# Starting a load-bound decode kernel: x and wq issued ahead of the start barrier, and the first key tile in two half loads behind fewer zero products

## The chip, the cores and the metric

The kernel runs on one core of one Trainium2 chip. Times are device microseconds (us) of a whole execution. The profile's span is about 1.4 us shorter than the time of the same execution. TensorE does the matrix products, VectorE and ScalarE copy, reduce and exponentiate, GpSimd fills constants, and SyncE issues nearly all loads, which 16 DMA engines carry out.

## The reference

```python
xn = layernorm(x)                                # x is [4, 1, 448]
s  = attention(xn, k_cache, v_cache, wq, wo)     # 16 query heads, 8 key/value heads, 8192 keys of 256
g  = silu(mlp_block(xn, w1, w2, w3, w4))         # with one token, the w1/w2 part is shifted out to zero
return x + s * g                                 # [4, 1, 448]
```

The caches are bfloat16 of shape [4, 8, 8192, 256]. So there are 32 tiles (batch, head), each with a key tile and a value tile of 4,194,304 bytes. The weights wq (3.67 MB), w3 and w4 (1.6 MB each) and wo (3.67 MB) come on top. Almost no arithmetic is done per byte.

## The kernel before

SyncE issues, in one queue: wq, w3, w4, key tiles 0 and 1, most of wo, then key tile 2, value tile 0, and so on. Key tile h waits until tile h-2 has been transposed (semaphore `v_k`), since it takes over its buffer. The first six loads, 18.0 MB, wait for nothing.

```python
def begin_ahead(nc, loads):             # moves these loads into the first block
    ...
    for load in reversed(loads):
        at = next(n for n, i in enumerate(first)
                  if i.engine == load.engine and isinstance(i, mybir.InstDrain))
        first.insert(at + 1, load)      # just behind the engine's drain of the start barrier

# SyncE
ahead.append(sp.sem_inc(S["pause"], 1)); ahead.append(take(sp, "pause"))
ahead.append(sp.dma_start(<wq>).then_inc(S["dwq"], 16))
...
load_k(0); load_k(1)
load_wo(NLATE, HQ, "dwo")
for h in range(2, NH):
    load_k(h)                           # waits for v_k >= h - 1
    load_v(h - 2)
# ScalarE
ahead.append(act.dma_start(x_sb[:, :], x2d).then_inc(S["dx"], 16))
```

TensorE first does the small layers (layernorm of x, then wq, w3, w4), then 14 products of zeros, which only keep it busy until key tile 0 has landed, then the tiles. A tile has 16 groups: 8 transposes of 128x128 (`f_t`), and three groups later the 8 score products (`f_s`). Its two tile bodies are a loop whose place in TensorE's program is set by `head_slot`, here 88.

```python
for i in range(NWARM):                  # 14
    pe.matmul(psv[0:PVW, 0:QW], pT[:, 0, 0:PVW], wq_sb[:, 0, 0:QW], start=True, stop=True)

def f_t(h, j):
    if j == 0:
        take(pe, "dk%d" % (h % 2), 16)  # the key tile has landed
    ...                                 # 8 transposes

with nc.Fori(0, 2, engines=[e]) as part:
    with nc.Fori(0, NH // 4, engines=[e], head_slot={e: 88}):
        body(0)
        body(1)
    with pe.If(part == 1):
        finish()
```

Of the kernel before, what the change touches and what calls it, by code (L numbers as in the profile page):

```python
# [12 lines left out]
P = 128  # L13
# [19 lines left out]
def begin_ahead(nc, loads):  # L33


    names = {i.name for i in loads}
    blocks = nc.main_func.blocks
    for b in blocks:
        rest = [i for i in b.instructions if i.name not in names]
        if len(rest) < len(b.instructions):  # L40
            b.instructions = rest
    first = blocks[0].instructions
    for load in reversed(loads):
        at = next(n for n, i in enumerate(first)
                  if i.engine == load.engine and isinstance(i, mybir.InstDrain))
        first.insert(at + 1, load)
    blocks[0].instructions = first


# [6 lines left out]
def bass_recurrent_scan__gqa_block_cached__mixer_s_mlp__decode_kernel(  # L56
# [32 lines left out]
    NCH = SK // P  # L89
# [5 lines left out]
    NGR = NCH // GC  # L95
# [15 lines left out]

    LATE = ((0, 1), (2,), (3,))
    NLATE = sum(len(g) for g in LATE)
    NWARM = 14
    ROW_PAD = 192
    TW = NHALF * REP
    OT_AHEAD = 3
# [3 lines left out]
    x2d = A_x.rearrange("b s d -> b (s d)")  # L121
# [3 lines left out]
    def where(h):  # L125
        return h // HKV, h % HKV

    with ExitStack() as es:
        def sb(name, shape, dty):
            return es.enter_context(nc.sbuf_tensor(name, shape, dty))  # L130

        align = sb("align", [P, ROW_PAD], BF16)
        kn = sb("kn", [P, 2, NCH, DH], BF16)
# [28 lines left out]
        x_sb = sb("x_sb", [Bn, D], BF16)  # L162
# [17 lines left out]
        psv = es.enter_context(nc.psum_tensor("psv", [P, 512], F32))  # L180

        S = {n: es.enter_context(nc.semaphore(n)) for n in (
            ["dx", "dwq", "dw3", "dw4", "dwo", "dk0", "dk1", "dv0", "dv1", "dout", "pause"]
            + ["dvl%d" % i for i in range(NPIECE)] + ["dwl%d" % i for i in range(len(LATE))]
            + ["p_td", "p_ta", "p_sc", "p_m1", "p_m2", "p_m3", "p_tr", "p_ou", "p_pv", "p_x", "p_q", "p_h", "p_h2", "p_o"]
            + ["v_ev", "a_ev", "v_rmax", "v_diag", "v_neg", "v_ot", "a_exp", "v_q", "g_c",
# [25 lines left out]
        def kn_dst(h):  # L212
            return kn[:, h % 2].rearrange("p c d -> p (c d)")

        def store(eng, i):
            eng.dma_start(out2d[:, i * DQ:(i + 1) * DQ], out_b[i * PQ:i * PQ + Bn, :]
                          ).then_inc(S["dout"], 16)

        def prog_sp(sp):
            ahead.append(sp.sem_inc(S["pause"], 1))  # L220
            ahead.append(take(sp, "pause"))
            ahead.append(sp.dma_start(
                vflat[1][:, 0:DK * HDH],
                A_wq.rearrange("d (t n) -> (d t) n", t=NHF).rearrange(
                    "(p j) n -> p (j n)", j=DK)).then_inc(S["dwq"], 16))
            sp.dma_start(vflat[0][:, 0:DK * FH],
                         B_w3.rearrange("d (t n) -> (d t) n", t=NHF).rearrange(
                             "(p j) n -> p (j n)", j=DK)).then_inc(S["dw3"], 16)
            sp.dma_start(w4_sb.rearrange("p a k n -> p a (k n)"),
                         B_w4.rearrange("(a p k) n -> p a (k n)", a=NHF, k=NFK)  # L230
                         ).then_inc(S["dw4"], 16)

            def load_k(h):
                b, g = where(h)
                if h >= 2:
                    sp.wait_ge(S["v_k"], h - 1)
                sp.dma_start(kn_dst(h), A_k_cache[b, g].rearrange("(p c) d -> p (c d)", p=P)
                             ).then_inc(S["dk%d" % (h % 2)], 16)

            def load_v(h):  # L240
                b, g = where(h)
                src = A_v_cache[b, g].rearrange("(p c) d -> p c d", p=P)
                if h < NH - 1:
                    sp.wait_ge(S["v_v"], h + 1)
                    sp.dma_start(vflat[h % 2], src.rearrange("p c d -> p (c d)")
                                 ).then_inc(S["dv%d" % (h % 2)], 16)
                else:

                    sp.wait_ge(S["v_k"], h)
                    for i in range(NPIECE):  # L250
                        lo, hi = PIECES[i], PIECES[i + 1]
                        sp.dma_start(
                            kn[:, 1 - h % 2, lo:hi, :].rearrange("p c d -> p (c d)"),
                            src[:, lo:hi, :].rearrange("p c d -> p (c d)")
                        ).then_inc(S["dvl%d" % i], 16)

            load_k(0)
            load_k(1)
            wo_src = A_wo.rearrange("(h p c) n -> p h (c n)", p=P, c=NHALF)

            def load_wo(lo, hi, sem):
                sp.dma_start(wo_sb[:, lo:hi].rearrange("p h c n -> p h (c n)"),
                             wo_src[:, lo:hi]).then_inc(S[sem], 16)

            load_wo(NLATE, HQ, "dwo")
            for h in range(2, NH):
                load_k(h)
                load_v(h - 2)
            load_v(NH - 2)
            load_v(NH - 1)  # L270
            for i, hs in enumerate(LATE):
                load_wo(hs[0], hs[-1] + 1, "dwl%d" % i)
            sp.wait_ge(S["v_out"], 1)
            store(sp, 0)
            take(sp, "dout", 16 * NDG)

        def take(eng, name, n=1):
            return eng.wait_ge(S[name], n).then_inc(S[name], -n)  # L278
# [23 lines left out]
        def evac(engine, h, j):  # L302
            take(engine, "p_td" if j in D_GROUPS else "p_ta")
            src = pst[j % NST][:].bitcast(BF16)
            dst = kT[:, j % RING, :]
            if j in D_GROUPS:
                engine.tensor_copy(dst, src).then_inc(S["v_ev"], 1)  # L307
            else:
                engine.activation(dst, src, ACT.Copy).then_inc(S["a_ev"], 1)  # L309

        def prog_act(act):
            ahead.append(act.dma_start(x_sb[:, :], x2d).then_inc(S["dx"], 16))
            c = _Chain(act, S["a_c"])
            for k, col in ((1, 0), (2, 8)):
                act.wait_ge(S["v_w"], k)
                c(act.activation(st[:, col + 2:col + 3], st[:, col + 1:col + 2], ACT.Sqrt))
            act.wait_ge(S["g_c"], NPC)
            for t in (vflat[1][:, DK * HDH:NCH * DH], vflat[0][:, DK * FH + NF * D:NCH * DH]):
                c(act.activation(t, pT[:, 0, 0:1].broadcast_to([P, t.shape[1]]), ACT.Copy))
            act.wait_ge(S["v_w"], 3)  # L320
            c(act.activation(gel_b[:, :], gel_a[:, :], ACT.Tanh))
            act.wait_ge(S["v_w"], 4)
            c(act.activation(sg4[:, :], bout[:, :], ACT.Tanh, scale=0.5))

            def exps(h):
                s = h % 2
                take(act, "v_neg")
                sc = psc[s][:, 0:NCH * REP].rearrange("p (k h) -> p k h", h=REP)
                pv_p = pT[:, s, 0:NCH * REP].rearrange("p (k h) -> p k h", h=REP)
                for hh in range(REP):  # L330
                    ins = act.activation(pv_p[:, :, hh], sc[:, :, hh], ACT.Exp,  # L331
                                         bias=negb[:, s, hh:hh + 1], scale=SCALE,
                                         accum_out=rowsum[:, s, hh:hh + 1])
                    if hh == REP - 1:
                        ins.then_inc(S["a_exp"], 1)

            with nc.Fori(0, NH // 2, engines=[mybir.EngineType.Activation]):
                for h in range(2):
                    for j in range(NGR):
                        if j not in D_GROUPS:  # L340
                            evac(act, h, j)
                        if j == J_BC + 2:
                            exps(h - 1)
            exps(NH - 1)
            act.wait_ge(S["v_out"], 1)
            store(act, 1)
# [200 lines left out]
        def prog_pe(pe, xn_mark, xn2_mark):  # L547
# [34 lines left out]
            for k in range(NFK):  # L582
                for a in range(NHF):
                    i = k * NHF + a
# [9 lines left out]

            for i in range(NWARM):
                pe.matmul(psv[0:PVW, 0:QW], pT[:, 0, 0:PVW], wq_sb[:, 0, 0:QW], start=True, stop=True)

            def f_t(h, j):
                if j == 0:
                    take(pe, "dk%d" % (h % 2), 16)  # L600
                dst = pst[j % NST][:].bitcast(BF16)
                for t in range(TB):
                    kl, half = divmod(t, NHALF)
                    ins = pe.transpose(dst[:, t * P:(t + 1) * P],  # L604
                                       kn[:, h % 2, GC * j + kl, half * P:(half + 1) * P],
                                       ident_b[:, :])
                ins.then_inc(S["p_td" if j in D_GROUPS else "p_ta"], 1)
# [70 lines left out]
            h = NH - 1  # L678
# [99 lines left out]
        marks, ahead = [], []  # L778
# [52 lines left out]
```

## Time and profile before

| what | value |
|---|---|
| time, median of the first 3 runs | 653.85 us (653.24 to 654.89) |
| span of the profiled run | 652.0 us |
| loaded from HBM | 279 MB, 428 GB/s over the span |
| TensorE busy, granted clock | 84%, 0.908 |

These are lines of the page. The DMA row gives, for 40 equal slices of the span, the busy share of the DMA engines in tenths (9 means 90% or more); the row below it gives GB/s.

```profile
span 652.0 us, 22813 instructions
...
DMA  9999999999999999999999999999999999999997
GB/s 374 440 420 433 430 434 434 430 438 426 440 426 440 426 440 426 440 428 436 432 435 430 434 434 426 440 426 440 426 440 428 438 428 438 430 436 430 434 429 301
```

The load stream is busy in every slice but part of the last. It is taken as the resource that bounds the kernel; run e7_2mb_less below tests that.

Next, the windows view at the start. The columns are the window, its length, the busy time of five engines, the TensorE clock, the busy share of the DMA engines and GB/s.

```profile
1.00:1.20 0.20, 0.00 (x0) 0.00 (x0) 0.20 (x1) 0.20 (x1) 0.07 (x1) 1.00 0.15 9
1.20:1.40 0.20, 0.00 (x0) 0.00 (x0) 0.20 (x1) 0.20 (x1) 0.10 (x1) 1.00 4.21 1008
...
2.20:2.40 0.20, 0.00 (x0) 0.00 (x0) 0.19 (x1) 0.00 (x0) 0.00 (x0) 1.00 0.00 0
```

The stream's packets begin at about 1.2 us (the 9 GB/s before that are x). A window books a packet whole where it starts. In this trace the first 16 packets of wq, 28 KB each, start between 1.26 and 2.12 us.

The timeline, from its parts for the start, for TensorE and for SyncE. Columns: start, length, engine, line, operation, out<-in, count, and in brackets the idle time just before and what ended it.

```profile
0.21 0.56 ACTq L312 DMA_DIRECT2D x_sb<-in_A_x_dram  x1
...
0.24 0.41 SPq L222 DMA_DIRECT2D vb<-in_A_wq_dram  x1
...
2.01 0.38 DVE L385 CAST x_f<-x_sb 4x448 f32<-4x448 bf16 x1 [0.60 <-DMA x_sb<-in_A_x_dram]
...
23.94 5.26 PE L596 MATMUL psv<-vb,pT 128*32 128x512 bf16 x14
30.07 1.05 PE L604 MATMUL pst<-ident_b,kn 128*128 128x128 bf16 x16 [0.87 <-PEq L278]
...
41.77 0.33 SPq L237 DMA_DIRECT2D kn<-in_A_k_cache_dram  x1
45.88 0.33 SPq L245 DMA_DIRECT2D vb<-in_A_v_cache_dram  x1
```

x is issued 0.03 us before wq; VectorE reads it at 2.0 us (L385). The zero products (L596) end at 29.2 us, and the first transposes (L604) start at 30.07 us after a pause of 0.87 us. Key tile 2 is issued at 41.77 us, value tile 0 at 45.88 us.

From the list of waits (total us, number, longest) and from the chain that ended last (start, length, what):

```profile
PE pst L604 <- PEq L278: 79.3, 29, 4.5
```

```profile
648.14 1.55 PE pst L703 x24
```

"PEq L278" is a semaphore wait in TensorE's own program; ahead of the first transpose of a tile (L604) it is the wait for the key tile. TensorE waits for key tiles in nearly every tile, 79.3 us in all. The execution ends with 24 output products, which wait for the last load of wo.

### The profile page before, as it was taken

What the parts mean: (1) busy time and instruction counts of PE and PEld (TensorE: products, weight loads), DVE (VectorE), ACT (ScalarE), POOL (GpSimd) and SP (SyncE); (2) the same over time, 40 slices, a digit from 0 to 9 for tenths busy, and PEclk for the clock granted to TensorE, in tenths of its full rate; (3) what the DMA queues carried; (4) which work ended last, traced back from release to release, by engine and by line L of the source; (5) the groups of instructions that cost most, each with busy time, mean ns of one, the idle gap of its engine ahead of it and who ended that gap; (6) DMA issues with size and microseconds to landing.
All of it is one profiled execution on the core that took longest, in us unless ns stands there. A gap on an engine that the chain in (4) does not pass through costs nothing. (4 is left out here: it accounts for less than half of the span.)

```text
span 652.0 us, 22813 instructions
## 1 busy us (share of the span) xinstructions
PE 550.5 (84%) x9937; PEld 470.7 (72%) x9937; DVE 276.9 (42%) x622; ACT 255.8 (39%) x364; POOL 3.6 (1%) x17
## 2 busy tenths in 40 slices
PE   2799997988887987888897888898888798878897
PEld 1487876987676876667787766787677688757774
DVE  7344544343343443434443444444344344434442
ACT  4144543443343443323443333444234344423440
POOL 2000000000000000000000000000000000000000
PEclk9998999888799898889987888988779987978999
DMA  9999999999999999999999999999999999999997
GB/s 374 440 420 433 430 434 434 430 438 426 440 426 440 426 440 426 440 428 436 432 435 430 434 434 426 440 426 440 426 440 428 438 428 438 430 436 430 434 429 301
DMA packets 12353, 279.13 MB, mean 428 GB/s; under 512 B 1204, under 2 KB 3256, under 8 KB 3768
## 3 DMA queue, kind: packets, MB, share of 16 engines
q1 hardware_dynamic: 12328, 278.99, 99.5%
q8 instruction: 7, 0.11, 0.1%
q10 hardware_dynamic: 16, 0.01, 0.0%
q14 instruction: 2, 0.02, 0.0%
HBM read 278.99 MB, written 0.00 MB: 428 GB/s over the span
## 5 line engine op out<-in xcount | busy, mean ns | idle before, releaser
L604 PE MATMUL pst<-ident_b,kn 128*128 128x128 bf16 x4096 | 342.7, 237 | 81.4 <-PEq L278 79.3
L309 ACT ACTIVATE kT<-pst 128x1024 bf16<-128x1024 bf16 x224 | 229.3, 1024 | 357.5 <-ACTq L278 356.3
L604 PEld LDWEIGHTS pst<-ident_b,kn 128*128 128x128 bf16 x4096 | 271.7, 107 | 87.2 <-issue 86.6
L307 DVE COPY kT<-pst 128x1024 bf16<-128x1024 bf16 x288 | 197.5, 691 | 261.1 <-DVEq L278 261.1
L616 PE MATMUL psc<-qc,kT 128*128 128x2 bf16 x4096 | 178.2, 164 | 0.0
L616 PEld LDWEIGHTS psc<-qc,kT 128*128 128x128 bf16 x4096 | 157.1, 98 | 28.7 <-issue 28.5
L655 PE MATMUL psv<-vb,pT 128*4 128x512 bf16 x1056 | 85.6, 378 | 0.0
L634 PE MATMUL psm<-sel,po 128*128 128x2 f32 x272 | 36.8, 257 | 0.5 <-PEq L278 0.5
L634 PEld LDWEIGHTS psm<-sel,po 128*128 128x128 f32 x272 | 34.8, 196 | 0.9 <-issue 0.9
L655 PEld LDWEIGHTS psv<-vb,pT 128*4 128x4 bf16 x1056 | 21.8, 82 | 15.0 <-issue 0.4
L466 DVE TENSOR_REDUCE rmax<-psc 128x2 f32<-128x128 f32 x32 | 9.3, 292 | 48.1 <-DVEq L278 48.1
L484 DVE COPY po<-psv 128x512 f32<-128x512 f32 x34 | 23.5, 691 | 4.0 <-DVEq L278 3.3
L331 ACT ACTIVATE pT<-psc,negb 128x64 bf16<-128x64 f32 x66 | 20.6, 332 | 5.4 <-ACTq L278 5.4
L471 DVE TENSOR_REDUCE gmax<-psm 2x1 f32<-2x128 f32 x32 | 8.9, 279 | 32.3 <-DVEq L278 32.3
L628 PEld LDWEIGHTS psm<-diag,ones_f 2*128 2x128 f32 x66 | 13.5, 253 | 6.3 <-issue 5.0
L628 PE MATMUL psm<-diag,ones_f 2*128 2x2 f32 x66 | 16.2, 313 | 1.1 <-PEq L278 0.9
L331 ACT ACTIVATION_READ_ACCUMULATOR pT<-psc,negb 128x1 f32 x66 | 13.6, 206 | 0.0
L624 PEld LDWEIGHTS psm<-ident_f,rmax 128*2 128x2 f32 x32 | 2.6, 80 | 14.0 <-issue 14.0
L646 PE MATMUL psm<-rowsum,ones_f 128*128 128x2 f32 x64 | 11.6, 251 | 0.0
L552 PE MATMUL pst<-ident_b,xn_b 4*128 4x4 bf16 x14 | 0.6, 161 | 11.5 <-DVE xn_b L379 6.8
L646 PEld LDWEIGHTS psm<-rowsum,ones_f 128*128 128x128 f32 x64 | 9.5, 188 | 0.0
L474 DVE TENSOR_SCALAR diag<-ident_f,gmax 2x2 f32<-2x2 f32 x32 | 6.9, 217 | 4.8 <-DVEq L278 1.1
(101 smaller groups left out, 101.1 us busy)
## 6 DMA issues: line engine op xcount, KB each, us to landing
kn<-in_A_k_cache_dram SPq DMA_DIRECT2D x32, 4096.0 KB, 25.5
vb<-in_A_v_cache_dram SPq DMA_DIRECT2D x31, 4096.0 KB, 30.5
vb<-in_A_wq_dram SPq DMA_DIRECT2D x1, 3584.0 KB, 11.4
vb<-in_B_w_dram SPq DMA_DIRECT2D x2, 1568.0 KB, 16.3
wo_sb<-in_A_wo_dram SPq DMA_DIRECT2D x1, 2688.0 KB, 43.3
kn<-in_A_v_cache_dram SPq DMA_DIRECT2D x1, 2048.0 KB, 24.7
kn<-in_A_v_cache_dram SPq DMA_DIRECT2D x1, 1024.0 KB, 26.7
kn<-in_A_v_cache_dram SPq DMA_DIRECT2D x2, 512.0 KB, 27.9
```

The source lines that it names most:

```text
L307: engine.tensor_copy(dst, src).then_inc(S["v_ev"], 1)
L309: engine.activation(dst, src, ACT.Copy).then_inc(S["a_ev"], 1)
L331: ins = act.activation(pv_p[:, :, hh], sc[:, :, hh], ACT.Exp, bias=negb[:, s, hh:hh + 1], scale=SCALE, accum_out=rowsum[:, s, hh:hh + 1])
L466: v.tensor_reduce(rmax[:, :], psc[h % 2][:, 0:NCH * REP].rearrange("p (k h) -> p h k", h=REP), AX.X, ALU.max).then_inc(S["v_rmax"], 1)
L471: v.tensor_reduce(gmax[:, :], psm[0:REP, 0:P], AX.X, ALU.max).then_inc(S["v_s"], 1)
L484: v.tensor_copy(po[:, slot], psv[:, 0:CP * DH]).then_inc(S["v_po"], 1)
L604: ins = pe.transpose(dst[:, t * P:(t + 1) * P], kn[:, h % 2, GC * j + kl, half * P:(half + 1) * P], ident_b[:, :])
L616: ins = pe.matmul(psc[h % 2][:, kk * REP:(kk + 1) * REP], kT[:, j % RING, t * P:(t + 1) * P], qc[:, h % 2, half, :], start=(half == 0), st ...
L628: pe.matmul(psm[:, P:P + REP], ones_f[0:REP, :], diag[:, :], start=True, stop=True).then_inc(S["p_m2"], 1)
L634: ins = pe.matmul(dst(dh)[:, 0:width], po[:, slot, i * DH + dh:(i + 1) * DH:NHALF], sel[:, i, 0:width], start=(i == 0), stop=(i == CP - 1))
L646: pe.matmul(psm[:, P + REP:P + 2 * REP], ones_f[:, :], rowsum[:, h % 2, :], start=True, stop=True)
L655: ins = pe.matmul(psv[o:o + CP * REP, 0:CP * DH], pT[:, h % 2, kk * REP:(kk + CP) * REP], src[:, kk:kk + CP, :].rearrange("p c d -> p (c d)"),
```

## The change

The intent is to start the stream and the prologue sooner: x and wq are issued before the start barrier, and TensorE begins on the first half of key tile 0 while the second half is in flight. Ten of the 14 zero products go, as the first half tile lands sooner than the whole one did. SyncE's inc-and-wait pair on `pause`, which only lets a little time pass, moves to the end. The diff, cut to its core:

```diff
 def begin_ahead(nc, loads):
...
+    for n, load in enumerate(loads):
+        ...                             # the first load (x) goes ahead of all its engine's work
+            at = first.index(drain)
+        first.insert(at, load)          # ahead of the drain, not behind it
-    NWARM = 14
+    NWARM = 4
...
-            ahead.append(sp.sem_inc(S["pause"], 1))      # both move to the end of SyncE's program
-            ahead.append(take(sp, "pause"))
-            ahead.append(sp.dma_start(<wq> ...
+            ahead.insert(1, sp.dma_start(<wq> ...
...
             def load_k(h):
+                if h == 0:
+                    src = A_k_cache[b, g].rearrange("(p c) d -> p c d", p=P)
+                    for i, sem in enumerate(("dk0", "dkh")):
+                        cs = slice(i * NCH // 2, (i + 1) * NCH // 2)
+                        sp.dma_start(<half i of kn[:, 0]>, <half i of src>).then_inc(S[sem], 16)
+                    return
...
-            ahead.append(act.dma_start(x_sb[:, :], x2d).then_inc(S["dx"], 16))
+            ahead.insert(0, act.dma_start(x_sb[:, :], x2d).then_inc(S["dx"], 16))
...
             def f_t(h, j):
                 if j == 0:
                     take(pe, "dk%d" % (h % 2), 16)
+                if j == NGR // 2 and h % 2 == 0:
+                    pe.wait_ge(S["dkh"], 16)
```

## The prediction

> **What bounds the kernel now.** The stream of loads from HBM on the 16 DMA engines. The page counts 279 MB in a span of 652.0 us; the DMA row reads 9 (90% or more) in 39 of 40 slices. The middle slices move 426 to 440 GB/s[...]. The list of waits agrees from the other side: TensorE waited 79.3 us in 29 places before a key tile's first transpose (2.7 us each), so it catches up with the stream in nearly every tile. The stream is unused only at its ends. At the front, windows of 0.2 us show no packet before 1.0 us and a hole from 2.2 to 2.8 us. At the back, the last packets come at 648.7 us; the chain that ended last is 24 output products from 648.14 us, two VectorE steps and the store.

> **What the change does, costed.**
> 1. x and wq go ahead of the start barrier's drain; SyncE's inc-and-wait pair goes to the end. The timeline shows the issues at 0.21 us (x) and 0.24 us (wq). Coming first, they start the stream at most about 0.2 us sooner. All else queues behind, so this is the only part on the critical path. The hole at 2.2 us is the stream filling; I expect it again.
> 2. Key tile 0 in two loads of 2 MB. Ahead of it are wq (3.67 MB), w3 and w4 (3.2 MB): the first half should be there at about 24 us (estimate: 9.0 MB at 430 GB/s plus 2 to 3 us of start), the second 5 us later. No byte is saved; the extra issue costs SyncE 0.35 us, far ahead of the queue.
> 3. Ten fewer zero products. The 14 took 5.26 us, until 29.2 us; four end near 25.4 us. The first transpose should start at about 26.3 us instead of 30.04 us. At some 0.65 us a group plus extras, TensorE reaches the middle of the tile near 32 us, with the second half landed: that wait costs about 0.
> 4. Tile 0 ends some 3.5 us sooner, so key tile 2 is issued near 38 us instead of 41.77 us and value tile 0 near 42 us instead of 45.88 us. But the loads before them (18 MB) keep the queue busy until about 46 us (wo landed 43.3 us after its issue at 2.92 us). Earlier issues only lengthen a queue that was not empty; TensorE's 3.5 us become a longer wait for key tile 2.
> 5. One more semaphore wait in each even tile, 0.05 us each: within TensorE's slack.

> **Prediction.** 653.85 us less about 0.3 us, with a spread of three runs of 653.2 to 654.9 us: 653.5 us, with 652.6 to 654.4 us holding it 8 times in 10. Faster by over 2%: 0.01; within 2%: 0.98; slower by over 2%: 0.01.

> **What would show each step.** (1) The wq issue near 0.1 us, first packets 0.1 to 0.2 us sooner. (2, 3) First transpose at 25 to 27 us, no wait of note in mid-tile. (4) Third key load issued near 38 us, DMA row still 9 throughout, last output products near 648 us, TensorE's total wait before key tiles up by 2 to 5 us.

> **What would make it wrong.** If the queue ran nearly dry at 42 to 46 us, where 405 GB/s may hide a small hole, early issues win 1 to 2 us. If x first fills the hole at 2.2 us, 0.6 us more. If half loads move bytes more slowly, a few tenths are lost.

## The result, and the profile after

Six runs of the changed kernel gave a median of 653.27 us (653.13 to 654.32). Six of the kernel before gave 653.73 us (653.24 to 654.89). The ratio is 0.9993, with a 95% interval of 0.9981 to 1.0006: the same. Here and below a ratio is the mean time of one kernel's runs over that of the other's in the same rounds, so it is not quite the ratio of the medians quoted. The changed kernel was run once more later (`after_again`, below): 0.9992, interval 0.9978 to 1.0005. Both point to a gain of 0.07 to 0.08%, and neither shows it apart from zero.

The same lines of the page, of the changed kernel:

```profile
span 651.9 us, 22794 instructions
...
DMA  9999999999999999999999999999999999999997
GB/s 379 440 418 438 423 442 426 440 428 434 434 432 436 426 440 420 446 422 444 424 441 426 438 430 434 434 432 436 424 440 422 444 424 442 426 442 426 438 428 299
```

The stream is as full as before. The windows at the start:

```profile
1.00:1.20 0.20, 0.00 (x0) 0.00 (x0) 0.00 (x0) 0.10 (x1) 0.10 (x1) 1.00 5.50 1290
...
2.20:2.40 0.20, 0.00 (x0) 0.00 (x0) 0.00 (x0) 0.18 (x1) 0.20 (x4) 1.00 0.00 0
```

The first packets of wq come 0.2 us sooner, in the window from 1.0 us. At 2.2 us again no packet starts, and again the first 16 are still running, until 2.70 us or later (2.86 us in the kernel before). The timeline:

```profile
0.00 0.40 SPq L228 DMA_DIRECT2D vb<-in_A_wq_dram  x1
0.12 0.56 ACTq L328 DMA_DIRECT2D x_sb<-in_A_x_dram  x1
...
4.92 0.38 DVE L401 CAST x_f<-x_sb 4x448 f32<-4x448 bf16 x1 [3.15 <-DMA x_sb<-in_A_x_dram]
...
26.36 1.91 PE L612 MATMUL psv<-vb,pT 128*32 128x512 bf16 x4
28.21 1.89 PE L622 MATMUL pst<-ident_b,kn 128*128 128x128 bf16 x16
...
41.65 0.33 SPq L251 DMA_DIRECT2D kn<-in_A_k_cache_dram  x1
45.75 0.33 SPq L259 DMA_DIRECT2D vb<-in_A_v_cache_dram  x1
```

wq is issued at 0.00 us, 0.24 us sooner. But x, at 0.12 us, now comes behind it, and VectorE gets x only at 4.92 us, 2.9 us later than before. The small layers all move back by that, so the zero products start at 26.36 us instead of 23.94 us. With 10 of them gone, the first transpose is at 28.21 us, only 1.9 us sooner than before. Its 16 transposes took 1.89 us instead of 1.05 us. In the end key tile 2 is issued at 41.65 us, 0.12 us sooner than before. The waits and the chain:

```profile
PE pst L622 <- PEq L294: 77.2, 28, 4.8
```

```profile
647.96 1.58 PE pst L721 x24
```

TensorE's waits for key tiles did not grow. The last 24 products start 0.18 us sooner, about what the stream's start gained.

One more line matters later: TensorE's timeline inside tile 0.

```profile
38.81 0.61 PE L622 MATMUL pst<-ident_b,kn 128*128 128x128 bf16 x8
39.96 0.35 PE L634 MATMUL psc<-qc,kT 128*128 128x2 bf16 x8 [0.54 <-issue]
```

Between these two groups TensorE stood still for 0.54 us with nothing in the profile to wait for ("issue"), after 204 products of the tile loop.

### The profile page after: what moved, and what is told of

It reads as the page before. It is cut to its first block, busy times and chain, and to the rows that moved or that the text cites. A ratio compares the mean times of both kernels' runs of the same rounds, so it can differ in the third digit from the quotient of the medians. Undisturbed runs are those within 1.5% of the kernel's fastest.

```text
span 651.9 us, 22794 instructions
## 1 busy us (share of the span) xinstructions
PE 550.5 (84%) x9927; PEld 472.3 (72%) x9927; DVE 276.8 (42%) x622; ACT 256.2 (39%) x364; POOL 3.6 (1%) x17
## 5 line engine op out<-in xcount | busy, mean ns | idle before, releaser
L622 PE MATMUL pst<-ident_b,kn 128*128 128x128 bf16 x4096 | 344.7, 238 | 78.2 <-PEq L294 77.2
L673 PE MATMUL psv<-vb,pT 128*4 128x512 bf16 x1056 | 87.2, 381 | 1.4 <-issue 1.4
## 6 DMA issues: line engine op xcount, KB each, us to landing
vb<-in_A_wq_dram SPq DMA_DIRECT2D x1, 3584.0 KB, 11.3
```

What stands on the lines that cost most here:

```text
L622: ins = pe.transpose(dst[:, t * P:(t + 1) * P], kn[:, h % 2, GC * j + kl, half * P:(half + 1) * P], ident_b[:, :])
L673: ins = pe.matmul(psv[o:o + CP * REP, 0:CP * DH], pT[:, h % 2, kk * REP:(kk + CP) * REP], src[:, kk:kk + CP, :].rearrange("p c d -> p (c d)"),
```

## The experiments

Theory A, mine: the stream bounds the kernel, so only its start counts. TensorE's early work counts only if key tile 2 is issued so late that the 18.0 MB ahead of it have run out. Rivals: TensorE's time saved in tile 0 is worth its full length (C); TensorE's slack absorbs any delay there (D). The times below are medians, beside the kernel before in the same rounds.

| run | edit | time, us | before, us | ratio, 95% interval | key tile 2 issued, us |
|---|---|---|---|---|---|
| e1_early_only | early issues only | 653.42 | 653.73 | 1.0007 (0.9993 to 1.0020) | 41.92 |
| e2_half_only | half loads, 4 zero products only | 653.96 | 653.73 | 1.0000 (0.9986 to 1.0013) | 40.72 |
| e3_x_first | changed, x ahead of wq | 653.75 | 653.73 | 1.0000 (0.9987 to 1.0014) | 41.32 |
| e4_wq_in_4 | changed, wq in 4 loads | 653.53 | 654.06 | 0.9994 (0.9983 to 1.0006) | 40.38 |
| e5_warm14 | changed, 14 zero products | 653.82 | 653.73 | 1.0009 (0.9995 to 1.0022) | 42.94 |
| e8_whole_wait | changed, waits for both halves | 654.37 | 654.06 | 1.0005 (0.9992 to 1.0018) | 43.20 |
| e6_warm34 | changed, 34 zero products | 662.25 | 654.06 | 1.0126 (1.0111 to 1.0141) | 48.10 |
| e7_2mb_less | changed, 2.1 MB less to load | 648.39 | 654.06 | 0.9919 (0.9904 to 0.9933) | 41.62 |
| e9_slot24 | e2 with another loop place | 661.88 | 654.25 | 1.0106 (1.0089 to 1.0123) | 43.26 |
| after_again | the changed kernel | 653.84 | 654.25 | 0.9992 (0.9978 to 1.0005) | 41.76 |
| e10_fill5 | changed, 5 fill products | 653.55 | 654.13 | 1.0002 (0.9987 to 1.0017) | 40.38 |
| e10_fill9 | changed, 9 fill products | 654.32 | 654.13 | 1.0005 (0.9992 to 1.0018) | 41.37 |

### Is it the stream? 2.1 MB less (e7_2mb_less)

```diff
+                if h == 16:             # only the first half of key tile 16; the rest is old data
+                    sp.wait_ge(S["v_k"], h - 1)
+                    sp.dma_start(<first half of kn[:, 0]>, <first half>).then_inc(S["dk0"], 16)
+                    return
```

> The changed kernel with only half of key tile 16 loaded (2.1 MB less; the second half is old data, so the result is wrong on purpose), nothing else changed and the same work on TensorE. Theory A: the time falls by 2.1 MB / 434 GB/s = 4.8 us, to about 648.5 us. If TensorE bounds the kernel: no change.

The time fell to 648.39 us. The changed kernel's medians, of other rounds, were 653.27 and 653.84 us, so this is 4.9 to 5.4 us less; the spans of the profiled runs went from 651.9 to 647.0 us, by 4.9 us. 2.097 MB in 4.9 us is 428 GB/s, the rate of the stream. TensorE's work was untouched. This is the plainest evidence for theory A. (The output still passed the comparison, although half of that tile's keys were wrong, so the comparison says little about this edit.)

### The two parts of the change, one at a time (e1_early_only, e2_half_only)

e1 is the changed kernel with these lines taken back:

```diff
-    NWARM = 4
+    NWARM = 14
-                if h == 0:  <two half loads>; return
-                if j == NGR // 2 and h % 2 == 0:
-                    pe.wait_ge(S["dkh"], 16)
```

> The changed kernel with key tile 0 in one load and 14 zero products again: only the early issues are left. Theory A (the load stream bounds the kernel; TensorE matters only if key tile 2 is issued after the 18 MB queued ahead of it have run out, which the bytes moved put at about 44.3 us): the stream starts 0.2 us sooner, but x still lands near 4.9 us, tile 0 starts near 33 us and key tile 2 is issued near 44.6 us, first packets 1.1 us later. So a hole of about 1 to 1.5 us in the stream and about 654.9 us, 1 us SLOWER than before. Theory B (the early start of the stream alone makes the gain): 653.4 us, as the changed kernel.

My expectation of a hole was wrong. x did land late (VectorE read it at 4.72 us), but the 14 zero products took 4.30 us instead of 5.26 us, and tile 0 started at 30.40 us, against 30.07 us before. Before, TensorE had paused for 0.87 us ahead of tile 0; the later prologue used up that pause. Key tile 2 was issued at 41.92 us, in time.

e2 is the other half: the kernel before with the two half loads, the wait in mid-tile and `NWARM = 4`, and nothing issued earlier.

> The kernel before with the half loads, the wait in mid-tile and 4 zero products, and nothing issued earlier. Theory A (stream-bound): x lands at 2.0 us as before, tile 0 starts at about 26.0 us, key tile 2 is issued near 38.5 us instead of 41.8 us, and the time is that of before, 653.7 us, within 0.3 us. Rival C (an earlier TensorE is worth its time): about 3 us faster, 650.5 us.

Its time was that of before, although tile 0 started at 25.83 us, 4.2 us sooner. But the second part of my expectation failed: key tile 2 was issued at 40.72 us and not near 38.5 us. So only 1.05 us of the 4.2 us was left by then, and what the run speaks against is C with a gain of 1 us (the interval allows 0.9 us at most), not with the 3 us that I had written. In e4 below 1.4 us was left, and the interval allows 1.1 us. TensorE's and SyncE's timelines of e2 show what held it:

```profile
35.52 0.61 PE L614 MATMUL pst<-ident_b,kn 128*128 128x128 bf16 x8
38.79 0.35 PE L626 MATMUL psc<-qc,kT 128*128 128x2 bf16 x8 [2.66 <-issue]
...
40.72 0.33 SPq L245 DMA_DIRECT2D kn<-in_A_k_cache_dram  x1
```

TensorE ran 4 us ahead, and then stood still for 2.66 us with no wait in the profile. The stop is at the same place in the program as in the changed kernel: after 204 products of the tile loop.

### Why x was late (e3_x_first, e4_wq_in_4)

```diff
 # e3: SyncE's pause pair, twice, ahead of the early wq; the pair at its end goes
-            ahead.insert(1, sp.dma_start(<wq>))
+            for _ in range(2):
+                ahead.append(sp.sem_inc(S["pause"], 1))
+                ahead.append(take(sp, "pause"))
+            ahead.append(sp.dma_start(<wq>))
 # e4: wq in four loads, each a quarter of every row
+            for i in range(4):
+                ahead.append(sp.dma_start(<quarter i of wq>).then_inc(S["dwq"], 16))
-            take(pe, "dwq", 16)
+            take(pe, "dwq", 64)
```

> The changed kernel with SyncE's inc-and-wait pair twice ahead of the early wq issue, so that x is issued first again. Theory A: wq is issued near 0.2 us, x lands near 2 us instead of 4.9 us, tile 0 starts near 25.5 us and key tile 2 is issued near 38.5 us; the time stays within 0.3 us of the changed kernel (653.3 us), as only the stream's start counts. Rival C: about 3 us faster than the changed kernel. If x still lands near 4.9 us, the order of issue is not what holds it up.

> The changed kernel with wq in four loads of a quarter of each row, so that one row of one load is 7 KB and not 28 KB. Theory A about x (it waits for some 2 to 3 of wq's long rows that are ahead of it on the same DMA engines; at 434 GB/s over 16 engines 28 KB take about 1.06 us, an estimate): x lands near 2.5 to 3 us instead of 4.9 us, key tile 2 is issued 2 us sooner than 41.65 us, and the time stays within 0.3 us of the changed kernel. Rival (x is late for the later end of the start barrier or for its own latency): x lands near 4.9 us again.

The timeline of e3, from its parts for the start and TensorE:

```profile
0.13 0.57 ACTq L329 DMA_DIRECT2D x_sb<-in_A_x_dram  x1
...
0.30 0.40 SPq L231 DMA_DIRECT2D vb<-in_A_wq_dram  x1
...
1.70 0.37 DVE L402 CAST x_f<-x_sb 4x448 f32<-4x448 bf16 x1
...
38.79 0.37 PE L635 MATMUL psc<-qc,kT 128*128 128x2 bf16 x8 [1.67 <-issue]
```

With x issued 0.17 us ahead of wq, x was there by 1.70 us. The start of e4:

```profile
0.00 2.04 SPq L230 DMA_DIRECT2D vb<-in_A_wq_dram  x4
0.12 0.56 ACTq L331 DMA_DIRECT2D x_sb<-in_A_x_dram  x1
...
3.03 0.37 DVE L404 CAST x_f<-x_sb 4x448 f32<-4x448 bf16 x1
```

With x behind wq again, but wq's rows cut from 28 KB to 7 KB, VectorE read x at 3.03 us without a wait. So x was held up by the long rows issued ahead of it, and 0.12 us in the order of issue cost it 2.9 us. The packets in the trace of the changed kernel show it directly: x's four packets of 896 bytes start at 2.70 to 3.46 us, when the first rows of wq are through, and the four that report its landing start at 3.83 to 4.58 us, 1.1 us after them, which is the time of one more row (1.07 to 1.16 us for the rows that start in between). Each of these eight packets starts within 4 ns of the end of a row of wq. In neither run did the time move. In e3 the loop reached its stop earlier and stood there for 1.67 us, again until 38.79 us.

### What the stop is (e9_slot24)

```diff
-                with nc.Fori(0, NH // 4, engines=[e], head_slot={e: 88}):     # on top of e2
+                with nc.Fori(0, NH // 4, engines=[e], head_slot={e: 24}):
```

> The kernel of half loads only (run e2_half_only) with TensorE's loop head placed at slot 24 of its 256-instruction block instead of slot 88, nothing else changed. Theory F: the stops of TensorE in its first pass (after 204 products of tile 0, 327 and 450 in all runs so far) are where its program crosses into a block of instructions that has not been fetched yet; a product is two instructions, so the stops move by 64 instructions, to about 235, 358 and 481 products, and the fetch of 0.02 MB is again seen about 2 us before the first stop ends. Rival (the stop is a wait for data or for another engine's semaphore): the stop stays at 204 products. In both cases the time is within 1 us of before, as the stream does not wait for it: key tile 2 is issued near 41 us.

TensorE's and SyncE's timelines of e9, and the line of the instruction queue (queue, packets, MB, share) of e9 and then of the changed kernel:

```profile
50.99 0.18 PE L626 MATMUL psc<-qc,kT 128*128 128x2 bf16 x1 [1.10 <-issue]
...
58.40 0.61 PE L614 MATMUL pst<-ident_b,kn 128*128 128x128 bf16 x8 [1.54 <-issue]
...
345.93 1.86 PE L614 MATMUL pst<-ident_b,kn 128*128 128x128 bf16 x16 [20.22 <-PEq L286]
...
322.36 0.33 SPq L245 DMA_DIRECT2D kn<-in_A_k_cache_dram  x1
...
359.89 0.33 SPq L245 DMA_DIRECT2D kn<-in_A_k_cache_dram  x1
```

```profile
q8 instruction: 16, 0.26, 0.2%
```

```profile
q8 instruction: 7, 0.11, 0.1%
```

The two later stops moved to 358 and 481 products, exactly as expected, and against e2 nothing else was edited. A packet of instructions starts between 48 and 49 us and one between 56 and 57 us, 1.4 to 3.0 us before these stops end at 50.99 and 58.40 us. So they are waits for instructions. (The first one, expected at 235, did not show: TensorE had already paused for 3.87 us at the head of the loop, and tile 0 started at 29.68 us.) What I did not expect was the time: 7.6 us slower by the medians of the same rounds. When the loop was entered for the second time, TensorE stood still for 20.22 us, until 345.93 us; 16 packets of instructions were fetched in all, not 7. Key tile loads came at 322.36 and then not before 359.89 us, and from 355 to 360 us the stream moved 62 GB/s.

The wait of 20.22 us is booked on the key tile's semaphore, but key tile 16 had landed at 327.64 us. What stood still was TensorE's branches. The loop's own branch in e9 and then in the changed kernel, number and min/median/max in ns, and last TensorE's timeline of e6, a run of the next section:

```profile
L782 PEldq COMPARE_BRANCH  x18: 76/208/6014, 23.5 to 642.2; - x18
```

```profile
L790 PEldq COMPARE_BRANCH  x18: 76/208/233, 26.0 to 633.4; - x18
```

```profile
341.73 1.86 PE L622 MATMUL pst<-ident_b,kn 128*128 128x128 bf16 x16 [13.62 <-PEq L294]
```

In e9 four branches took over 5 us: one of 6.01 us at the first entry, which is the pause before tile 0, and 6.65, 7.68 and 5.84 us from 325 us on, at the second entry. In the changed kernel the same three took 0.35, 0.22 and 0.18 us. Of all the kept traces only that of e6 shows the like, with 17 packets of instructions and branches of 7.85 and 5.30 us at the second entry, and there the loop is at slot 88. So the slot alone does not decide it: 30 more products ahead of the loop do the same, and 10 more (e5) do not. What decides it is open.

### How much slack TensorE had (e5_warm14, e8_whole_wait, e6_warm34)

```diff
-    NWARM = 4                                          # e5 and e6
+    NWARM = 14                                         # e5;  34 in e6
-                if j == NGR // 2 and h % 2 == 0:       # e8
+                if j == 0 and h % 2 == 0:
                     pe.wait_ge(S["dkh"], 16)
```

> The changed kernel with 14 zero products in place of 4 (10 more of 0.38 us). Theory A: tile 0 starts near 32 us, its first 16 transposes take 1.05 us as before and not 1.9 us, key tile 2 is issued near 44.2 us, at the edge of the queue running out: 0.5 to 1.5 us slower than the changed kernel, about 654.3 us. Rival D (TensorE's slack of 2.7 us a tile absorbs it): 653.3 us.

> The changed kernel with the wait for the second half load moved to the start of the tile, so that the half loads serve nothing. Theory A: the second half lands near 29.5 us, so tile 0 starts near 29.7 us instead of 28.2 us, key tile 2 is issued near 43 us instead of 41.65 us, packets near 44.1 us, just before the queue would run out: the time stays within 0.4 us of the changed kernel, 653.3 to 653.7 us. Rival C: 1.5 us slower, 654.8 us.

> The changed kernel with 34 zero products in place of 4 (30 more of 0.38 us, 11.3 us). Theory A (the stream runs out near 44.3 us whatever TensorE does): key tile 2 is issued near 51.7 us, the stream has a hole of about 8.4 us near 44 to 53 us that nothing later makes good, and the time is about 661.7 us. Rival D (TensorE's slack makes it good later): within 2 us of the changed kernel. Rival C (TensorE's time counts in full): 11.3 us slower, 664.6 us.

In e6 key tile 2 was issued at 48.10 us. Its windows:

```profile
44.00:45.00 1.00, 1.00 (x28) 1.00 (x26) 0.79 (x3) 0.73 (x2) 0.00 (x0) 1.00 0.51 188
45.00:46.00 1.00, 0.86 (x20) 0.68 (x17) 0.74 (x2) 0.73 (x2) 0.00 (x0) 1.00 0.08 29
46.00:47.00 1.00, 0.59 (x15) 0.59 (x16) 0.09 (x1) 1.00 (x1) 0.00 (x0) 1.00 0.00 0
...
48.00:49.00 1.00, 1.00 (x23) 0.53 (x21) 0.72 (x2) 0.00 (x0) 0.00 (x0) 1.00 0.06 16
49.00:50.00 1.00, 1.00 (x22) 0.53 (x21) 0.00 (x0) 0.00 (x0) 0.00 (x0) 1.00 1.86 524
```

The queue was running dry from 44 us and empty by 46 us, and full packets came again about 1 us after the issue. At 43.20 us (e8) a dip shows:

```profile
45.00:46.00 1.00, 1.00 (x26) 0.47 (x22) 0.36 (x2) 0.00 (x0) 0.00 (x0) 1.00 0.41 165
```

From 45 to 46 us e8 moves 165 GB/s, where the changed kernel moves 495. With each packet spread over the time it took, e8 has loaded 0.29 MB less than the changed kernel by 50 us, 0.7 us of the stream, and still does at 600 us. e5, at 42.94 us, moves 364 GB/s in that microsecond and loses 0.15 MB. e1, at 41.92 us, loses nothing. So key tile 2 has to be issued before about 42 to 43 us: the kernel before, at 41.77 us, had at most 1.2 us to spare, and the changed kernel 1.3 us. The times do not tell e8 or e5 apart from before. But e8's five runs lie at 654.28 to 654.64 us and not at 653.3 to 653.7 us as I expected, closer to the 654.8 us of rival C. The loss in the stream accounts for 0.7 us of that; in its profile TensorE was also late at the end, as in the next section. In e5 key tile 2 came 1.3 us sooner than I expected.

e6 took 8.2 us more than the kernel before in the same rounds, and 8.4 to 9.0 us more than the changed kernel's medians of other rounds. That is close to the 8.4 us that I expected, but the sum behind it was wrong. The 34 zero products took 9.45 us (0.28 us each, not 0.38 us), so key tile 2 came at 48.10 us and not at 51.7 us. By 60 us the stream was 2.2 MB behind the changed kernel (summed from windows of 1 us), about 5.1 us at 433 GB/s. Another 0.4 MB, about 0.9 us, went between 325 and 400 us, around the 13.62 us that TensorE stood still at the second entry; so e6 is not a test of the early hole alone. The rest came at the end: the rate fell from 335 to 23 GB/s over the 5 us from 652 to 657 us, where the changed kernel went from 383 to 41 GB/s in 3 us. Why the engines finish so unevenly there is open (e9, whose stream also ran dry, ends in the same way). In any case nothing later made the hole good, which rules out D.

### The spread at the end (after_again, e10_fill5, e10_fill9)

> The changed kernel once more, unedited, to see how far two executions of one program differ in the start of the last 24 products and in the span. Theory A: within 0.3 us of before in the mean of the rounds, 653.1 to 654.3 us in the single runs; the first packets again at 1.0 to 1.1 us.

The first packets were again in the window from 1.0 us, but the span was 652.9 us, 1.0 us longer than in the first profile of this program. So two executions of one program differ by five times what the change can gain. In this profile, the last 24 products follow other products without a pause: TensorE was late. So it was in the profiles of e2, e4 and e8. Over the last tile its clock was low, 0.82 to 0.85 in all four; the window of the last tile:

```profile
618.00:636.00 18.00, 17.25 (x301) 15.12 (x301) 7.18 (x16) 7.77 (x11) 0.00 (x0) 0.84 1.00 430
```

I tried to take that away with zero products before every odd tile, to keep TensorE busy while it waits.

```diff
             def body(h):
+                for _ in range(5 if h == 1 else 0):          # 9 in e10_fill9
+                    pe.matmul(psc[h][0:PVW, :], <zeros of pT>, kT[:, RING - 1, 0:512], start=True, stop=True)
```

> The changed kernel with 5 more zero products of 512 columns (about 0.22 us each at full clock) on TensorE ahead of every odd key tile, so also in its wait before the last tile. So far single runs lie between 653.2 and 655 us, and in the profiles that end late (spans 652.6 to 653.2) TensorE's granted clock over the last tile, 618 to 636 us, is 0.82 to 0.85 and TensorE has no pause before its last 24 products; where the clock is 0.91 to 1.00 the span is 651.7 to 652.2. Theory G (the spread of a microsecond is TensorE's clock after its idle wait for the last key tile): the clock over the last tile is 0.9 or more, TensorE waits for the last wo load again, and the single runs lie at 653.1 to 653.5 us, narrower than the changed kernel's 653.1 to 654.3. Rival (the spread comes from the load stream): the single runs spread as before. If the 10 more instructions shift a block of TensorE's program as in run e9_slot24, several us are lost and the fetches in the page go up from 7.

> The same with 9 zero products, about 1.9 us, as long as TensorE's wait before the last tile (1.8 to 3.1 us). Theory G: the clock over the last tile is 0.95 or more, single runs at 653.1 to 653.5 us. Rival: as for e10_fill5.

```profile
618.00:636.00 18.00, 16.32 (x318) 13.86 (x319) 8.13 (x18) 8.32 (x15) 0.00 (x0) 1.00 1.00 433
```

The five zero products took 1.25 us and the nine 2.12 us, so 0.22 us for each further one. The line is that of e10_fill9; the clock over the last tile was 1.00 in both, and TensorE again waited for the last load of wo (0.42 and 0.43 us). That agrees with the cause I gave for the low clock, on one profile each (the kernel before and e5 also read 1.00, without the fill). But the single runs still spread from 653.24 to 656.37 us (e10_fill5) and from 653.57 to 655.41 us (e10_fill9). In e10_fill9 the last key tile started at 618.74 us, against 617.67 us in the first profile of the changed kernel, and TensorE had waited for it for 0.93 us after its nine products: the key tile itself came late. With each packet spread over the time it took, this execution had loaded 0.3 MB less by 200 us than the first one of the changed kernel, 0.7 us of the stream, and never made it good. So theory G falls as the whole explanation of the spread: in four profiles TensorE was the late party, in this one the stream, and why the stream falls behind is open. Neither version is told apart from the kernel before.

## Why the prediction was right or wrong

- **The bound: right.** Taking away 2.1 MB took away 4.9 us of the span, which is 428 GB/s.
- **Step 1, the early issues: right in its size, not shown by the times.** wq was issued 0.24 us sooner, the packets came 0.2 us sooner, the last products started 0.18 us sooner in the first profile. The runs agree with 0.3 us (ratios 0.9993 and 0.9992) but also with zero. The packets are clearer: spread over the time they took, at 300 us they put the changed kernel 0.08 MB ahead of the kernel before and e1 (early issues only) 0.09 MB, about 0.2 us of the stream, and e2 (no early issues) 0.00 MB. So the gain in the stream is there in these traces and comes from the early issues; the spread at the end hides it. Step 1 missed a side effect: x went behind wq and landed 2.9 us later.
- **Step 2: right.** There was no wait in mid-tile, and the half loads by themselves (e2) cost and gained nothing that the runs show.
- **Step 3, "the first transpose should start at about 26.3 us": wrong.** It was 28.21 us. The step took the prologue's times from the kernel before, although the same change moved x. In e2, where x keeps its place, it was 25.83 us. Nor had I counted that the first 16 transposes could run more slowly: from start to start most take 106 to 107 ns in the changed kernel and 55 to 56 ns in the kernel before (118 and 66 ns each when the 1.89 and 1.05 us are divided by 16). The trace of the changed kernel has both paces later on, with the clock: 106 to 107 ns for most from 61.66 to 65.07 us, where its record says 0.50, and 55 to 56 ns from there to 112.86 us, where it says 1.00. At the start the pace changes where the first clock record (1.00) begins, at 30.94 us in the changed kernel, among its second 16 transposes, and at 28.14 us in the kernel before, among its zero products, which went from 427 to 216 ns. The windows view reads a clock of 1.00 from 28 to 30 us of the changed kernel, but its trace has no record there, so that reading says nothing. What sets the moment of the change was not tested. (e2, also with 4 zero products, lay between: 1.23 us for 16.)
- **Step 4, "key tile 2 is issued near 38 us": wrong in size, right in its conclusion.** It was 41.65 us. Of the 3.65 us between them, 1.9 us is the later start of tile 0, 1.2 us the slower products at its beginning, and 0.54 us the stop. And had x kept its place, TensorE would have been stopped in mid-tile for instructions until 38.79 us, as e2 and e3 were. "Earlier issues only lengthen a queue that was not empty" held: in e2 and e4 key tile 2 came about 1 us sooner and the time did not move. The waits of TensorE did not go up by 2 to 5 us (77.2 after 79.3 us), as there was hardly an early finish to be waited out.
- **Step 5: consistent, not isolated.** TensorE's semaphore instructions take 51 ns each in the traces of both kernels, and TensorE had more waits than that to spare.
- **What would have made it wrong.** The queue was not dry before, but it was nearer to it than the prediction knew: at most 1.2 us was left. The hole at 2.2 us was none, and having x first (e3) gave no measured gain.

The whole came out right because the steps that failed all lay behind the slack of the queue. The evidence does not say that they were small: 2.9 us in x, 2.7 us in a stop. That the 2.9 us of x, which the prediction did not foresee, fitted into a slack of about 1 us was luck and not its working. The total itself is weak evidence, as an unchanged time lies in the predicted range too.

## What to carry to other kernels

In a kernel bound by its load stream, ask of every saving at the start only whether it moves the first byte or keeps the queue from running dry; here a tile that started 4.2 us sooner (e2) gained nothing that the runs show, with 18.0 MB queued ahead of the next load. When a small load and a large one are moved together, look at which is issued first: here a load of 3.5 KB, issued 0.12 us behind rows of 28 KB, came 2.9 us later. When an engine stops with no wait in the profile, count instructions from the loop's head; here the stops (0.54 to 2.66 us) stayed at fixed counts and moved with the loop's place, and were waits for the program itself. Look at the durations of its branches too: in e6 and e9 the waits of 13.62 and 20.22 us that the profile books on a semaphore held branches of 5.30 to 7.85 us.
